# Sliding-window decode attention with a gated feed-forward on one core: TensorE's jumps out, wq in two transfers, four rows of wo moved, a jump announced on VectorE

## The chip, the cores and the metric

The kernel runs on one core of a Trainium2 chip. The metric is the device time of one execution in microseconds (us), lower is better. The profile is of one execution of its own, with its own time.

## The reference

`D` is 448, there are two batch rows (`B`), 16 query heads, 8 key/value heads and a head size of 256. Only the last 2048 rows of the caches are used. Everything in memory is bf16.

```python
def _A_ref(x, k_cache, v_cache, wq, wo):
    ...
    q = (lambda x, *d: x.transpose(*d))((x @ wq).reshape(B, Sq, Hq, Dh), 0, 2, 1, 3)
    k = jnp.repeat(k_cache[:, :, Sk - W:, :], rep, axis=1)
    v = jnp.repeat(v_cache[:, :, Sk - W:, :], rep, axis=1)
    scores = jnp.einsum("bhqd,bhkd->bhqk", q, k) * (Dh ** -0.5)
    p = _softmax(scores, axis=-1)
    o = jnp.einsum("bhqk,bhkd->bhqd", p, v)
    return (lambda x, *d: x.transpose(*d))(o, 0, 2, 1, 3).reshape(B, Sq, Hq * Dh) @ wo
...
xn = _layernorm(x, axis=-1)
s = _A_ref(xn, A_k_cache, A_v_cache, A_wq, A_wo)
g = _silu(_B_ref(xn, B_w1, B_w2))     # relu(xn @ w1) @ w2
return x + s * g
```

## The kernel before, in words

The work is 44.1 MB of reading: wq (3.67 MB), w1 and w2 (1.6 MB each), 16.8 MB of keys, 16.8 MB of values and wo (3.67 MB). A tile is always 128 partitions; the weights lie so that each partition gets one contiguous run of the source (`wq_src`, `w1_src`, `w2_src`, `wo_src`, L234 to L237). wo's partition p holds rows 32p to 32p+31 of the matrix, so a "row j" below means one row of 448 elements (896 bytes) in each of the 128 partitions.

**Order of the work.** A small recorder, `_Prog`, collects operations in five lists, one for each engine, with the operations that each depends on. `run` (L43) writes the lists out and turns dependences into semaphore waits. An engine's order is the order of the calls; nothing else plans it. All operations pass through `op` and `dma`, so the trace gives L39 for transfers and L294 for all matmuls.

**SyncE** issues all large transfers, in this order: wq (L241), w1, w2, the four key blocks of 4.2 MB (`d_k`, L245, `u` = 0 to 3), then the value blocks (`load_v`, L460). A value block goes into the same buffer `kv[u]` as the keys, so it waits for the last score matmul of that block (`last_S[u]`). The fourth one is cut in halves (L481 and L482). Last comes wo in five pieces of 20, 4, 4, 3 and 1 rows (`WO_PARTS`, L147; issued at L500) into `wqo`, the buffer that held wq. **ScalarE's queue** issues the three small loads of x (`x_sb` at L231, `x_c` at L233), before ScalarE's own work.

**Start.** VectorE makes the layernorm from `x_sb` (L254 to L291); TensorE turns it (`mbk`, L297) and VectorE writes `xr` (L300). TensorE multiplies with wq (`qbk`, L305 to L311). VectorE and TensorE bring the queries into `qstat` (L312 to L325). Then `do_H` and `do_F` do the feed-forward, and VectorE keeps `g_sb` (L457).

**Middle.** For each block, `do_turn` transposes the keys on VectorE, `do_S` multiplies, `do_max` and the exponential follow, `do_et` transposes. After `do_spread`, `do_PV(u)` multiplies with the values, `do_out` normalises and `do_turn_out` brings the result into `at2`. `fill` (L385) is TensorE work whose result nobody reads.

**End.** Rows 0 to 23 of wo are multiplied into `wbk` with four rows side by side in the array (L505), and VectorE copies the sum (`wc`, L510). Rows 24 to 31 go as four narrow matmuls each into `fbk` (L513); before row 28 (`WO_FOLD`) the sum `wc` is added in (L514 to L518). VectorE multiplies with `g_sb` (L527), adds x (L529), and two stores go out (L531).

**Jumps.** `emit_pe` (L79) cuts TensorE's list at four marks and puts the parts in bodies. TensorE starts with `eng.br("visit1")`, jumps on to `visit3`, from there back to `part0` at the start of its list, then runs the parts in order with a jump between them. A register that is never set decides every conditional jump the same way. `mark_branch_hint_location` and `branch_hint` put an instruction ahead that tells the sequencer of a later jump.

Of the kernel before, what the change touches and what calls it, by code (L numbers as in the profile page):

```python
# [22 lines left out]
class _Prog:  # L23
# [5 lines left out]

    def mark(self, name, more=0):  # L30
        self.marks[name] = len(self.lists[PE]) + more

# [10 lines left out]
    def run(self):  # L43
# [30 lines left out]

        for eng, e in ((nc.sync, SP), (nc.gpsimd, POOL), (nc.scalar, ACTE), (nc.vector, DVE)):
            emit(eng, self.lists[e])
        self.emit_pe(emit)

    def emit_pe(self, emit):  # L79


        nc, eng, ops, seen = self.nc, self.nc.tensor, self.lists[PE], {}
        a, b, c, d = (self.marks[k] for k in ("block1", "block2", "block3", "late"))

        def body(name):
            return nc.body(name, valid_engines=[eng.engine])

        zero = eng.alloc_register("never_set")
        eng.br("visit1")
        with body("part0"):  # L90
            emit(eng, ops[:a], seen)
            eng.br("part1")
        with body("visit1"):
            eng.reg_mov(zero, 0)
            told_visit = eng.mark_branch_hint_location()
            eng.br("visit3")
        with body("part1"):
            emit(eng, ops[a:b], seen)
            told_late = eng.mark_branch_hint_location()
            emit(eng, ops[b:c], seen)  # L100
            eng.br("part3")
        with body("visit3"):
            eng.br_eq(zero, 0, "part0", "part3").branch_hint(told_visit)
        with body("part3"):
            emit(eng, ops[c:d], seen)
            eng.br_eq(zero, 0, "late", "over").branch_hint(told_late)
        with body("over"):
            eng.br("late")
        with body("late"):
            eng.br_eq(zero, 0, "part4", "past")  # L110
        with body("past"):
            eng.br("part4")
        with body("part4"):
            emit(eng, ops[d:], seen)


def bass_recurrent_scan__sliding_block_cached__dense_activation_relu__decode_kernel(
# [28 lines left out]
    PADW = 5  # L146
    WO_PARTS = [20, 4, 4, 3, 1]  # L147
    WO_TILED = 24
    WO_FOLD = 28

    es = contextlib.ExitStack()
    with es:
        pr = _Prog(nc, es)

        def named(name, shape, dt):
            return es.enter_context(nc.sbuf_tensor(name, shape, dt))
# [56 lines left out]
        o_odd = named("o_odd", [128, DH], F32)  # L213
        at2 = named("at2", [128, 32 * PADW], BF)

        sbk = [psum(f"sbk{i}", [128, 512], F32) for i in range(2)]
# [7 lines left out]
        def half(t, h):  # L224
            return t.rearrange("b s (k h n) -> h (b s k) n", h=2, n=NCOL)[h]
# [4 lines left out]

        d_x = pr.dma(ACTE, x_sb[0:B, :], A_x[:, 0, :])  # L231
        p_xc = pr.op(POOL, lambda e: e.memset(x_c[:, :], 0.0))
        d_xc = [pr.dma(ACTE, x_c[32 * h:32 * h + 4, :], half(A_x, h), [p_xc]) for h in range(2)]  # L233
        wq_src = A_wq.rearrange("r (hf c) -> (r hf) c", hf=2).rearrange("(p s) c -> p (s c)", s=SLOTS)  # L234
# [5 lines left out]
        st = {}  # L240
        d_wq = pr.dma(SP, wqo[:, 0:SLOTS * HC], wq_src)  # L241
        st["w1"] = pr.dma(SP, w1_sb[:, :], w1_src)
        st["w2"] = pr.dma(SP, w2_sb[:, :], w2_src)
        for u in range(NU):
# [6 lines left out]
        p_z = [pr.op(POOL, lambda e, t=t: e.memset(t[:, :], 0.0))  # L251
               for t in (fpad, asel, rm, bt, qstat, at2)][-1]

        v_bn = pr.op(DVE, lambda e: e.bn_stats(st6[0:B, :], x_sb[0:B, :]), [d_x])  # L254
# [8 lines left out]
        def z(t):  # L263
            return a_z[t.name]
# [39 lines left out]

        deps = [d_wq, v_xr, z(qbk)]  # L305
        for s in range(SLOTS):
# [132 lines left out]
        def do_F():  # L439
            deps = [st["w2"], st["h"], z(fbk)]  # L440
            for j in range(14):
                i = j % 4
                o = pr.op(PE, mm(fbk[32 * i:32 * i + B, 0:D], h_sb[:, 32 * j:32 * j + 2], w2_sb[:, j * D:j * D + D],
                                 j < 4, j >= 10, tile_position=(0, 32 * i)), deps)
                deps = []
            v = pr.op(DVE, lambda e: e.tensor_copy(zc[:, :], fbk[:, 0:D]), [o])
            deps = [v, v_fp, st["mbk"]]
# [21 lines left out]
        pr.mark("block1", 16)  # L469
        do_S(1)  # L470
# [17 lines left out]
        for u in range(NU):  # L488
            do_PV(u)
            if u == 0:  # L490
                pr.mark("block2")
# [10 lines left out]
        pr.mark("block3")  # L502
        fill(2)
        deps = [st["at"], z(wbk)]
        for j in range(WO_TILED):  # L505
            i = j % 4
            o = pr.op(PE, mm(wbk[32 * i:32 * i + B, 0:D], view(at2, PADW * j + 1, [[2, B]]), wqo[:, j * D:j * D + D],
                             j < 4, j >= WO_TILED - 4, tile_position=(0, 32 * i)), deps + [landed.get(j)])
            deps = []
        v_wc = pr.op(DVE, lambda e: e.tensor_copy(wc[:, :], wbk[:, 0:D]), [o])  # L510
        pr.mark("late")
        deps = [st["g"]]
        for j in range(WO_TILED, 32):  # L513
            if j == WO_FOLD:  # L514
# [4 lines left out]
            for c in range(4):  # L519
                k, h = divmod(c, 2)  # L520
                lo = j * D + c * NCOL
                m_o = pr.op(PE, mm(fbk[32 * h:32 * h + 4, 0:NCOL], at2[:, PADW * j + 1 - k:PADW * j + 5 - k],
                                   wqo[:, lo:lo + NCOL], j == WO_TILED and k == 0, j == 31,
                                   tile_position=(0, 32 * h)), deps + [landed.get(j)])
                deps = []

        v_t = pr.op(DVE, lambda e: e.tensor_tensor(  # L527
            out=tmp[0:ROWS, :], in0=fbk[0:ROWS, 0:NCOL], in1=g_sb[0:ROWS, :], op=ALU.mult), [m_o, st["g"]])
# [35 lines left out]
```

## Time and profile before

| | us |
|---|---|
| median of 3 runs (109.98 to 110.4) | 110.16 |
| the profiled execution's own time | 110.08 |
| its span, first to last instruction of the program | 108.8 |
| matmuls, busy | 59.0 |
| VectorE, busy | 61.5 |
| ScalarE, busy | 9.0 |
| mean rate read from HBM over the span | 406 GB/s |

Times are counted from the start of the span. Busy shares are averages over stages with different limits: what counts is which wait ends last in a stage. Besides instructions the trace keeps DMA packets (start, duration, size, queue), and for each transfer the moments at which its semaphore rises, one for each of the DMA engines that carry it; a transfer over 128 partitions has sixteen. Packets on queues named "instruction" bring program code to an engine's sequencer: they are not issued by any line of the kernel.

### The profile page before, as it was taken

How to read it: one execution, taken by the hardware profiler on the slowest of the kernel's cores; microseconds unless marked ns; L12 is line 12 of the kernel's file. 1: busy time of each engine (PE TensorE's matmuls, PEld its weight loads, DVE VectorE, ACT ScalarE, POOL GpSimd, SP SyncE). 2: the span in 40 equal slices, each digit the busy share in tenths (PEclk: the TensorE clock that was granted, in tenths of full speed). 3: DMA queues.
4: the chain of work that ended last, by engine and by line, in shares of the span. 5: the costliest groups of instructions: out<-in, count | busy, mean ns of one | idle time of the engine just before them, and what ended most of it. 6: DMA issues, size and time to landing. Idle time of an engine off the chain costs nothing.

```text
span 108.8 us, 1114 instructions
## 1 busy us (share of the span) xinstructions
PE 59.0 (54%) x469; PEld 15.1 (14%) x469; DVE 61.5 (57%) x84; ACT 9.0 (8%) x18; POOL 2.1 (2%) x13
## 2 busy tenths in 40 slices
PE   0001295650000069919961996299538967779672
PEld 0000023120000011001100120012023222313131
DVE  2920007634099979999999999940449332304021
ACT  2970000000000000002000200020020000000000
POOL 7000000000000000000000000000000000000000
PEclk9999999995555558995998599669955699999999
DMA  6899999989998999899999999999999899999960
GB/s 165 337 428 411 409 434 507 407 386 494 458 398 386 494 446 410 386 494 446 410 389 482 446 410 398 470 458 410 398 458 470 362 428 434 434 422 422 397 254 1
DMA packets 2488, 44.17 MB, mean 406 GB/s; under 512 B 306, under 2 KB 436, under 8 KB 820
## 3 DMA queue, kind: packets, MB, share of 16 engines
q1 hardware_dynamic: 2456, 44.11, 95.2%
q8 instruction: 3, 0.05, 0.2%
q10 hardware_dynamic: 28, 0.00, 0.0%
q14 instruction: 1, 0.01, 0.0%
HBM read 44.11 MB, written 0.00 MB: 406 GB/s over the span
## 4 chain that ended last, share of the span: by engine, by line
DMA 56%; DVE 28%; PE 8%; SPq 5%; issue 1%
DMA kv<-in_A_k_cache_dram 32%; DVE kv L329 24%; DMA wqo<-in_A_wo_dram 23%; PE sbk L294 7%; SPq L39 5%; PE fbk L294 1%; DVE q_x L358 1%; DVE rm L346 1%; DVE rm_t L348 0%; DVE bias L352 0%; DVE bt L349 0%; DVE tmp L527 0%; DVE out_sb L529 0%
## 5 line engine op out<-in xcount | busy, mean ns | idle before, releaser
L294 PE MATMUL sbk<-kv,qstat 128*8 128x512 bf16 x128 | 30.2, 1092 | 22.9 <-DVE kv L329 22.9
L329 DVE STREAM_TRANSPOSE kv<-kv 128x2048 f32<-128x2048 f32 x16 | 35.6, 2276 | 4.6 <-DMA kv<-in_A_k_cache_dram 4.6
L294 PEld LDWEIGHTS sbk<-kv,qstat 128*8 128x8 bf16 x128 | 4.5, 107 | 46.9 <-DVE kv L329 28.9
L294 PE MATMUL obk<-kv,pt 128*16 128x512 bf16 x128 | 9.5, 442 | 2.5 <-DVE xg L410 1.2
L407 DVE TENSOR_SCALAR o_odd<-obk,rs 128x256 f32<-128x256 f32 x4 | 1.9, 484 | 11.0 <-PE obk L294 11.0
L353 ACT ACTIVATE e_sb<-sbk,bias 128x512 bf16<-128x512 f32 x4 | 2.8, 688 | 51.9 <-DVE bias L352 51.9
L294 PE MATMUL sbk<-kv,f 128*8 128x512 f32 x14 | 6.9, 612 | 0.0
L294 PE MATMUL qbk<-wqo,xr 128*4 128x512 bf16 x28 | 3.2, 625 | 4.2 <-DMA wqo<-in_A_wq_dram 4.2
L346 DVE TENSOR_REDUCE rm<-sbk 128x1 f32<-128x512 f32 x4 | 2.7, 663 | 4.8 <-PE sbk L294 4.8
L294 PE MATMUL mbk<-ident,xg 2*128 2x2 bf16 x7 | 0.3, 160 | 8.5 <-issue 8.5
L312 DVE TENSOR_SCALAR q_x<-qbk 128x512 bf16<-128x512 f32 x1 | 0.7, 691 | 7.1 <-PE qbk L294 7.1
L294 PEld LDWEIGHTS obk<-kv,pt 128*16 128x16 bf16 x128 | 3.2, 97 | 8.5 <-issue 5.0
L358 DVE STREAM_TRANSPOSE q_x<-e_sb 128x512 bf16<-128x512 bf16 x4 | 2.8, 692 | 1.7 <-ACT e_sb L353 1.7
L375 DVE TENSOR_TENSOR pt<-spk,pmask 128x512 bf16<-128x512 f32 x4 | 2.6, 684 | 0.8 <-PE spk L294 0.8
L510 DVE COPY wc<-wbk 128x448 f32<-128x448 f32 x1 | 0.6, 625 | 3.8 <-PE wbk L294 3.8
L294 PE MATMUL qbk<-w_sb,xr 128*2 128x448 bf16 x28 | 2.8, 572 | 0.0
L294 PE MATMUL spk<-q_x,perm 128*32 128x128 bf16 x16 | 0.7, 298 | 3.1 <-DVE q_x L358 3.1
L323 DVE CAST qstat<-mbk 32x256 bf16<-32x256 f32 x4 | 1.7, 420 | 0.7 <-PE mbk L294 0.7
L410 DVE SCALAR_TENSOR_TENSOR xg<-obk,rs,o_odd 128x256 bf16<-128x256 f32 x4 | 1.9, 484 | 0.1
L294 PE MATMUL wbk<-wqo,at 128*2 128x448 bf16 x24 | 1.4, 351 | 1.0 <-DMA wqo<-in_A_wo_dram 1.0
L254 DVE BATCH_NORM_STATS2 st<-x_sb 2x6 f32<-2x448 bf16 x1 | 0.6, 615 | 2.1 <-DMA x_sb<-in_A_x_dram 2.1
L294 PE MATMUL fbk<-w_sb,h_sb 128*2 128x448 bf16 x14 | 0.9, 351 | 1.5 <-issue 1.5
(72 smaller groups left out, 33.4 us busy)
## 6 DMA issues: line engine op xcount, KB each, us to landing
kv<-in_A_k_cache_dram SPq DMA_DIRECT2D x4, 4096.0 KB, 39.7
kv<-in_A_v_cache_dram SPq DMA_DIRECT2D x3, 4096.0 KB, 22.2
kv<-in_A_v_cache_dram SPq DMA_DIRECT2D x2, 2048.0 KB, 17.5
wqo<-in_A_wq_dram SPq DMA_DIRECT2D x1, 3584.0 KB, 12.2
w_sb<-in_B_w_dram SPq DMA_DIRECT2D x2, 1568.0 KB, 17.0
wqo<-in_A_wo_dram SPq DMA_DIRECT2D x1, 2240.0 KB, 24.3
wqo<-in_A_wo_dram SPq DMA_DIRECT2D x2, 448.0 KB, 25.1
wqo<-in_A_wo_dram SPq DMA_DIRECT2D x1, 336.0 KB, 25.8
```

Source lines behind the costliest of these rows:

```text
L39: o = _Op(eng, lambda e: e.dma_start(dst, src), [d for d in deps if d is not None], True)
L254: v_bn = pr.op(DVE, lambda e: e.bn_stats(st6[0:B, :], x_sb[0:B, :]), [d_x])
L294: return lambda e: e.matmul(out_ap, lhsT=lhsT, rhs=rhs, start=start, stop=stop, skip_group_check=True, **kw)
L312: v_q = pr.op(DVE, lambda e: e.tensor_scalar(out=view(q_x, 0, [[256, 8], [128, 2], [1, 32]]), in0=view(qbk, 0, [[64, 8], [1, 2], [2, 32]]) ...
L323: st["q"] = st["mbk"] = pr.op(DVE, lambda e, Q=Q: e.tensor_copy(qstat[32 * Q:32 * Q + 32, 256 * Q:256 * Q + 256], mbk[32 * Q:32 * Q + 32, ...
L329: st["turn", u] = pr.op(DVE, lambda e, n=n: e.transpose(kf[:, 2048 * n:2048 * n + 2048], kf[:, 2048 * n:2048 * n + 2048]), [d_k[u]])
L346: v = pr.op(DVE, lambda e: e.tensor_reduce(out=rm[:, 0:1], in_=sbk[u % 2][:, :], axis=AX.X, op=ALU.max), [last_S[u], p_z, st.get(("rmt", u ...
L353: st["exp", u] = pr.op(ACTE, lambda e: e.activation(e_sb[:, :], sbk[u % 2][:, :], ACT.Exp, bias=bias[:, 0:1], accum_out=ssum[:, u:u + 1]), ...
L358: st["et", u] = pr.op(DVE, lambda e: e.transpose(q_x[:, 512 * u:512 * u + 512], e_sb[:, :]), [st["exp", u], m_qt])
L375: st["pt", u] = pr.op(DVE, lambda e: e.tensor_tensor(out=view(pt[u], 0, [[8, 64], [2, 4], [1, 2]]), in0=view(spk, 128 * u, [[2, 64], [0, 4 ...
L407: v = pr.op(DVE, lambda e: e.tensor_scalar(out=o_odd[:, :], in0=obk[:, DH:2 * DH], scalar1=rs[:, 2 * u + 1:2 * u + 2], scalar2=None, op0=A ...
L410: st["osb", u] = pr.op(DVE, lambda e: e.scalar_tensor_tensor(out=o_sb[:, lo:lo + DH], in0=obk[:, 0:DH], scalar=rs[:, 2 * u:2 * u + 1], in1 ...
```

## The change

- **TensorE** loses all jumps; its list is written out straight. `emit_pe` is gone.
- **wq** comes by two transfers: slots 0 to 3 from SyncE, slots 4 to 6 from ScalarE's queue. The second is now first in ScalarE's queue, and the loads of x come behind it.
- **wo**: of the 32 rows of each partition the first 28 stay in `wqo`, in pieces of 18, 4, 3, 2 and 1. The last four go into partitions 32 to 79 of three places: those of source partitions 0 to 47 to a free part of `wqo`, 48 to 95 to `w1_sb`, 96 to 127 to `w2_sb` (48, 48 and 32 partitions of 3584 bytes). These three transfers are issued ahead of the rest of wo. Their other operand, `atx`, is made from `at2` by three matmuls with 0/1 matrices (`move`) and a copy. The matmuls with them (12, three for each four rows) come first in `wbk`. Rows 0 to 21 follow there; rows 22 to 27 go the narrow way, with the fold before row 25.
- **VectorE** makes `move` with three copies after `do_F`, announces a jump right behind them, before the first `do_turn`, and jumps between its last `wc` copy and its last two operations. GpSimd clears `move`.

```diff
-    def mark(self, name, more=0):
-        self.marks[name] = len(self.lists[PE]) + more
+    def mark(self, name):
+        self.marks[name] = len(self.lists[DVE])
...
-        for eng, e in ((nc.sync, SP), (nc.gpsimd, POOL), (nc.scalar, ACTE), (nc.vector, DVE)):
+        for eng, e in ((nc.sync, SP), (nc.gpsimd, POOL), (nc.scalar, ACTE), (nc.tensor, PE)):
             emit(eng, self.lists[e])
-        self.emit_pe(emit)
+        self.emit_dve(emit)
+    def emit_dve(self, emit):
+        nc, eng, ops, seen = self.nc, self.nc.vector, self.lists[DVE], {}
+        a, b = self.marks["tell"], self.marks["jump"]
+        emit(eng, ops[:a], seen)
+        zero = eng.alloc_register("never_set")
+        eng.reg_mov(zero, 0)
+        told = eng.mark_branch_hint_location()
+        emit(eng, ops[a:b], seen)
+        eng.br_eq(zero, 0, "last", "past").branch_hint(told)
+        with nc.body("past", valid_engines=[eng.engine]):
+            eng.br("last")
+        with nc.body("last", valid_engines=[eng.engine]):
+            emit(eng, ops[b:], seen)
...
-    WO_PARTS = [20, 4, 4, 3, 1]
-    WO_TILED = 24
-    WO_FOLD = 28
+    WO_PARTS = [18, 4, 3, 2, 1]
+    WO_ALL = sum(WO_PARTS)
+    WO_EXTRA = 32 - WO_ALL
+    WO_MOVED = ((0, 12), (48, 12), (96, 8))
+    WO_TILED = 22
+    WO_FOLD = 25
...
-        d_wq = pr.dma(SP, wqo[:, 0:SLOTS * HC], wq_src)
+        d_wq = [pr.dma(eng, wqo[:, lo * HC:hi * HC], wq_src[:, lo * HC:hi * HC])
+                for eng, lo, hi in ((SP, 0, 4), (ACTE, 4, SLOTS))]
+        d_x = pr.dma(ACTE, x_sb[0:B, :], A_x[:, 0, :])
+        d_xc = [pr.dma(ACTE, x_c[32 * h:32 * h + 4, :], half(A_x, h), [p_xc]) for h in range(2)]
...
+            if hg == 0:
+                return
+            deps = [st["at"], v_mv]
+            for x in range(len(WO_MOVED)):
+                at_x = 352 + x * WO_EXTRA * B
+                o = pr.op(PE, mm(mbk[:, at_x:at_x + WO_EXTRA * B], move[:, 128 * x:128 * x + 128],
+                                 view(at2, PADW * WO_ALL + 1, [[PADW, WO_EXTRA], [2, B]]), True, True), deps)
+                deps = []
+            st["atx"] = st["mbk"] = pr.op(DVE, lambda e: e.tensor_copy(
+                atx[:, :], mbk[:, 352:352 + len(WO_MOVED) * WO_EXTRA * B]), [o])
...
+        for x, (q, nq) in enumerate(WO_MOVED):
+            v_mv = pr.op(DVE, lambda e, x=x, q=q, nq=nq: e.tensor_copy(
+                view(move, 128 * x + 32, [[4, nq], [1, 4]]), view(ident, q, [[1, nq], [nq, 4]])), [p_id, p_mv])
+        pr.mark("tell")
...
+        moved = [t[:, lo:lo + WO_EXTRA * D] for t, lo in ((wqo, WO_ALL * D), (w1_sb, 0), (w2_sb, 0))]
         landed, j0 = {}, 0
         for n in WO_PARTS:
+            if j0 == 0:
+                for x, (q, nq) in enumerate(WO_MOVED):
+                    src = wo_src[q:q + 4 * nq, WO_ALL * D:].rearrange("(r q) c -> q r c", r=4)
+                    landed["x", x] = pr.dma(SP, moved[x][32:32 + 4 * nq, :], src, [m_q, st["h"], st["f"]])
             landed[j0] = pr.dma(SP, wqo[:, j0 * D:(j0 + n) * D], wo_src[:, j0 * D:(j0 + n) * D], [m_q])
```

More of the change, by code (lines that the diff above doesn't have):

```diff
@@ L73, in emit @@
                     made.then_inc(o.sem, 16 if o.dma else 1)
-        for eng, e in ((nc.sync, SP), (nc.gpsimd, POOL), (nc.scalar, ACTE), (nc.vector, DVE)):
+        for eng, e in ((nc.sync, SP), (nc.gpsimd, POOL), (nc.scalar, ACTE), (nc.tensor, PE)):
             emit(eng, self.lists[e])
-        self.emit_pe(emit)
[L79 to L86, printed above, removed]
-        zero = eng.alloc_register("never_set")
[L89 to L114, printed above, removed]
+        self.emit_dve(emit)
[3 more added lines that the diff above has]
+        emit(eng, ops[:a], seen)
+        zero = eng.alloc_register("never_set")
+        eng.reg_mov(zero, 0)
[6 more added lines that the diff above has]
+            emit(eng, ops[b:], seen)
 def bass_recurrent_scan__sliding_block_cached__dense_activation_relu__decode_kernel(
@@ L214, in bass_recurrent_scan__sliding_block_cached__dense_activation_relu__decode_kernel @@
         at2 = named("at2", [128, 32 * PADW], BF)
+        atx = named("atx", [128, len(WO_MOVED) * WO_EXTRA * 2], BF)
+        move = named("move", [128, len(WO_MOVED) * 128], BF)
         sbk = [psum(f"sbk{i}", [128, 512], F32) for i in range(2)]
@@ L229, in kv_src @@
             return cache[b, 4 * hg:4 * hg + 4, SK - W:SK, :].rearrange("g (p t) d -> p g (t d)", t=NT)
-        d_x = pr.dma(ACTE, x_sb[0:B, :], A_x[:, 0, :])
         p_xc = pr.op(POOL, lambda e: e.memset(x_c[:, :], 0.0))
-        d_xc = [pr.dma(ACTE, x_c[32 * h:32 * h + 4, :], half(A_x, h), [p_xc]) for h in range(2)]
         wq_src = A_wq.rearrange("r (hf c) -> (r hf) c", hf=2).rearrange("(p s) c -> p (s c)", s=SLOTS)
@@ L252, in bass_recurrent_scan__sliding_block_cached__dense_activation_relu__decode_kernel @@
                for t in (fpad, asel, rm, bt, qstat, at2)][-1]
+        p_mv = pr.op(POOL, lambda e: e.memset(move[:, :], 0.0))
         v_bn = pr.op(DVE, lambda e: e.bn_stats(st6[0:B, :], x_sb[0:B, :]), [d_x])
@@ L302, in bass_recurrent_scan__sliding_block_cached__dense_activation_relu__decode_kernel @@
             in1=view(par8, 0, [[1, SLOTS], [1, 2], [0, 2]]), op=ALU.mult), [m_xr, v_par8])
-        deps = [d_wq, v_xr, z(qbk)]
+        deps = d_wq + [v_xr, z(qbk)]
         for s in range(SLOTS):
@@ L445, in do_F @@
                 deps = []
+            st["f"] = o
             v = pr.op(DVE, lambda e: e.tensor_copy(zc[:, :], fbk[:, 0:D]), [o])
@@ L468, in bass_recurrent_scan__sliding_block_cached__dense_activation_relu__decode_kernel @@
         do_turn(1, 0, 4)
-        pr.mark("block1", 16)
         do_S(1)
@@ L489, in bass_recurrent_scan__sliding_block_cached__dense_activation_relu__decode_kernel @@
             do_PV(u)
-            if u == 0:
-                pr.mark("block2")
             if u in (0, NU - 1):
@@ L496, in bass_recurrent_scan__sliding_block_cached__dense_activation_relu__decode_kernel @@
                 do_turn_out(u - 2)
+        moved = [t[:, lo:lo + WO_EXTRA * D] for t, lo in ((wqo, WO_ALL * D), (w1_sb, 0), (w2_sb, 0))]
         landed, j0 = {}, 0
         for n in WO_PARTS:
+            if j0 == 0:
+                for x, (q, nq) in enumerate(WO_MOVED):
+                    src = wo_src[q:q + 4 * nq, WO_ALL * D:].rearrange("(r q) c -> q r c", r=4)
+                    landed["x", x] = pr.dma(SP, moved[x][32:32 + 4 * nq, :], src, [m_q, st["h"], st["f"]])
             landed[j0] = pr.dma(SP, wqo[:, j0 * D:(j0 + n) * D], wo_src[:, j0 * D:(j0 + n) * D], [m_q])
             j0 += n
-        pr.mark("block3")
         fill(2)
-        deps = [st["at"], z(wbk)]
-        for j in range(WO_TILED):
-            i = j % 4
-            o = pr.op(PE, mm(wbk[32 * i:32 * i + B, 0:D], view(at2, PADW * j + 1, [[2, B]]), wqo[:, j * D:j * D + D],
-                             j < 4, j >= WO_TILED - 4, tile_position=(0, 32 * i)), deps + [landed.get(j)])
+        rows = []
+        for x in range(len(WO_MOVED)):
+            for j in range(WO_EXTRA):
+                k = B * len(rows)
+                rows.append((atx[:, k:k + B], moved[x][:, j * D:j * D + D], landed["x", x]))
+        for j in range(WO_TILED):
+            rows.append((view(at2, PADW * j + 1, [[2, B]]), wqo[:, j * D:j * D + D], landed.get(j)))
+        deps = [st["at"], st["atx"], z(wbk)]
+        for k, (lhsT, rhs, d) in enumerate(rows):
+            i = k % 4
+            o = pr.op(PE, mm(wbk[32 * i:32 * i + B, 0:D], lhsT, rhs, k < 4, k >= len(rows) - 4,
+                             tile_position=(0, 32 * i)), deps + [d])
             deps = []
         v_wc = pr.op(DVE, lambda e: e.tensor_copy(wc[:, :], wbk[:, 0:D]), [o])
-        pr.mark("late")
         deps = [st["g"]]
-        for j in range(WO_TILED, 32):
+        for j in range(WO_TILED, WO_ALL):
             if j == WO_FOLD:
@@ L522, in bass_recurrent_scan__sliding_block_cached__dense_activation_relu__decode_kernel @@
                 m_o = pr.op(PE, mm(fbk[32 * h:32 * h + 4, 0:NCOL], at2[:, PADW * j + 1 - k:PADW * j + 5 - k],
-                                   wqo[:, lo:lo + NCOL], j == WO_TILED and k == 0, j == 31,
+                                   wqo[:, lo:lo + NCOL], j == WO_TILED and k == 0, j == WO_ALL - 1,
                                    tile_position=(0, 32 * h)), deps + [landed.get(j)])
                 deps = []
+        pr.mark("jump")
         v_t = pr.op(DVE, lambda e: e.tensor_tensor(
```

## The prediction

> **What bounds the kernel now.** I read the page first: the slices, the DMA queues, the chain.
>
> ```profile
> span 108.8 us, 1114 instructions
> ...
> DMA  6899999989998999899999999999999899999960
> ...
> q1 hardware_dynamic: 2456, 44.11, 95.2%
> q8 instruction: 3, 0.05, 0.2%
> ...
> q14 instruction: 1, 0.01, 0.0%
> ```
>
> The DMA digits are 8 or 9 from the second slice to the 38th: SyncE's queue (q1) keeps its sixteen engines busy for 95.2% of the span, and TensorE and VectorE only have to keep up. They do: each value block is issued (46.48, 56.17, 66.93, 77.57) some 10 us before the queue has worked off what is ahead of it. Packet by packet the trace shows the same: a 32768-byte packet takes 1.213 us with no gap behind it on every engine. So the end is set by bytes per DMA engine, and by the last engine, not the mean one.
>
> Then the start and the end of the timeline (start, duration, engine):
>
> ```profile
> 2.08 0.61 DVE L254 BATCH_NORM_STATS2 st<-x_sb 2x6 f32<-2x448 bf16 x1 [2.08 <-DMA x_sb<-in_A_x_dram]
> ...
> 8.84 0.19 DVE L300 TENSOR_TENSOR xr<-mbk,par 128x28 bf16<-128x28 f32 x1 [2.67 <-PE mbk L294]
> ...
> 12.96 3.16 PE L294 MATMUL qbk<-wqo,xr 128*4 128x512 bf16 x28 [4.16 <-DMA wqo<-in_A_wq_dram]
> ```
>
> ```profile
> 104.62 0.62 DVE L510 COPY wc<-wbk 128x448 f32<-128x448 f32 x1 [3.82 <-PE wbk L294]
> ...
> 105.34 0.56 PE L294 MATMUL fbk<-wqo,at 128*4 128x112 bf16 x16 [0.78 <-DMA wqo<-in_A_wo_dram]
> ...
> 105.73 0.55 PE L294 MATMUL fbk<-wc,fpad 128*4 128x112 f32 x8
> ...
> 106.19 0.56 PE L294 MATMUL fbk<-wqo,at 128*4 128x112 bf16 x16
> 106.79 0.27 DVE L527 TENSOR_TENSOR tmp<-fbk,g_sb 36x112 f32<-36x112 f32 x1 [1.54 <-PE fbk L294]
> ```
>
> At the start, x is there at 2 and wq at 12.9. At the end TensorE waits for pieces of wo, and all that follows is a tail of 2.4 us.
>
> The semaphore of the last piece of wo rises sixteen times: thirteen engines between 104.94 and 105.52, then 105.79, 106.22 and 106.39. Three are late because they also carried program code. Two carried TensorE's (16384 bytes at 1.93 in 1.48 us, at 5.79 in 0.96); the packet behind each took 1.53 instead of 1.06. On wq these two were 0.8 and 1.0 late already, and kept that. The third carried 8192 bytes at 54.79 (0.31 us, next packet 1.74 instead of 1.21: 0.84 lost). A last 16384 bytes came at 105.62, when they no longer hurt. Laid end to end the packets tell something of the engines: the two small loads of x_c, four partitions each, ran on the same four engines. The one late from 54.79 is one of those four; the two of TensorE's code are not.
>
> **Part by part**, against the profiled execution's 110.08 (0.08 below the median of 110.16).
>
> *TensorE's jumps out.* Seven jumps (318, 6607, 256, 178, 190, 218 and 349 ns), one move and two hints go. Gain: 0. The 6.6 us jump hides under the wait for wq at 12.96, the last two under waits for wo. What moves is the code: TensorE gets it where it reaches it. The second body began at 48.7; its end, and with it the next block, was due at about 85, the last at 100. From jump to going on took 6.6 us under a full queue, and there are 36 and 15 us of cover: 0, and at most 6.6 without it. The engines pay as before: 0.96 plus 0.47 for each block. If the one of 105.62 is asked for at 100, one more engine pays 1.4.
>
> *wq in two.* The bytes are the same. SyncE's first issue took 0.41 us and its first packets began at 1.76, 1.0 after it; ScalarE's queue began at 1.66, so both start together. The first packets took 1.70 to 2.32 instead of 1.07: two queues could hide up to 0.65 of that; or, if a change of queue costs what it cost behind the code blocks, lose 0.5. The row nearest is x_c, which alternated with wq at no cost (next packet 1.08): 0, with both ends kept. That the first packets are 16384 bytes instead of 28672 narrows their spread: engines ended the first packet between 3.53 and 4.10, that 0.58 stayed to the end (104.94 to 105.52), and 0.57 of it is 0.33.
>
> *x behind wq.* x_sb now waits in ScalarE's queue behind eight packets of 12288 bytes an engine (0.46 each), which alternate with eight of 16384 (0.61): 1.77 + 0.65 + 8 × 1.07 = 11.0, then two packets of w1 at 0.47 and 0.3 for the semaphore: 12.2 instead of 2.06. From x to `xr` there are 3.4 us of instructions without their waits (0.61, 0.17, 0.14, 0.20, 0.14, 1.26, the matmuls, 0.19, gaps): 15.6. The wq matmuls start at 15.7 instead of 12.96, 2.7 late; `g_sb` ends at 28.9 instead of 26.2. The three copies for `move` (0.26 each, the row of `perm`) end at 29.7. The first `do_turn` began at 30.02, when the last, late engine had landed the keys; the others landed by 29.07. So it begins about 29.8: 0. Without this cover, VectorE's chain still has the 10 us ahead of the value loads. GpSimd's clearing (0.36 by the row of `qstat`) meets nothing.
>
> *Moved rows.* Loads of two, four and 128 partitions ran on two, four and sixteen engines. Sources of 12, 12 and 8 outer steps should then run on 12, 12 and 8, that is four packets of 3584 bytes for each engine and transfer. Until now each engine had eight of them for these rows, at 0.136 us. So eight engines get four more (+0.55), four keep theirs, and four lose all eight (-1.09). The Trainium skill, "DMA: Bandwidth & Descriptors", section "Why a DMA increments its semaphore by 16 and not by 1", gives the rule: the largest count up to 16 that divides the slowest dimension of both sides, and the lowest-numbered engines; the two loads of x agree with it (two and four engines), and no run yet shows a twelve. If all sixteen shared instead, the end would stay where it is.
> The sum: unloaded engines that carried code end at 106.39 - 1.09 = 105.30. Loaded ones end at 104.94 plus their own offset (0 to 0.33, 0.2 taken) plus 0.55 plus 0.03 for three more completions: 105.72. The last landing goes from 106.39 to 105.72, a gain of 0.67. This takes the two TensorE engines to be among the relieved four; of twelve engines that they can be, these are the only ones where the edit pays.
>
> *The moved rows on the engines.* Behind the last `at2` copy (ends 100.8) stand three matmuls (0.2); the fills, four matmuls at 0.43, wait for them and end at 102.7 instead of 102.1; the copy `atx` (0.33) is done by 101.4. Twelve rows take three rounds of four at 0.19, to 103.3. The first big piece has landed by then (twelve rows behind it took 3.31, ten take 2.76: 105.72 - 2.76 = 103.0); its 18 rows and the next four, landed at 104.05, take 5.5 rounds, and the last matmul 0.35: 104.7. `wc` ends at 105.3. Rows 22 to 24 have gone through by then; the fold takes 0.46, the last three rows 0.29, the last matmul 0.21: 106.25. Before, the last matmul ended 0.36 after the last landing, now 0.5: the tail gives back 0.1. If `wc` comes 0.3 later, so does the end: this is now the nearest thing behind the landing.
>
> *VectorE's jump.* The 8 KB at 54.79 would sit on an engine that now also carries 0.55 more: 105.79 + 0.58 = 106.37, no gain at all. TensorE's second hint (82.55) was followed by no code packet until its jumps at 104.21 and 104.5, so I take an announced jump to keep the next block away till then. The jump itself took 0.18 to 0.35 in the rows above; VectorE idles 1.54 before L527, so 0. In the Trainium skill, "Runtime: NRT & Kernel Launch", section "Instruction fetch mechanics", a taken branch out of the resident window waits for a fetch, and straight code does not. The 6.6 us jump shows such a wait here; by the rule VectorE would pay at its last jump, a rival below.
>
> Sum: -0.67 + 0.1 = -0.57: 110.08 to **109.5**.
>
> **The rivals.**
> - *Both queues start faster*: another 0.3 to 0.65 off, 109.0. For it: the slow first packets. Against: the engine with two kinds of packets at 1.93 was slower at both.
> - *The code comes to VectorE anyway, or sixteen engines share the moved rows*: the last landing stays at 106.37, 110.1.
> - *The relief falls on the wrong engines* (slower): TensorE's code on an engine with +0.55: 106.39 + 0.58 = 106.97, so 110.7. The same if the third block is fetched at 100 on a loaded engine. It decides as soon as one of the code engines lies among the eight. For: nothing in the trace names the two, only that they are not of the first four.
> - *VectorE's last jump waits for code* (slower): asked at about 105.4, 1.1 until the packet (104.5 to 105.62 on TensorE), 0.31, and 1.25 from packet to going on (6.75 to 8.0): 108.1 instead of 106.4, so 111.2. It decides once the wait exceeds 1.0. For: the 6.6 us jump. Against: six other jumps at 0.18 to 0.35.
> - *Each change of queue in wq costs 0.47* (slower): eight times, 3.8, so 113.3. Against: x_c.
>
> **How the numbers follow.** Forecast 0.50, with its own range of 109.2 to 109.8; 0.35 of it lies below 109.5, roughly 0.5% under the time before (0.5% is about what a measurement of this kernel can tell from no change), 0.15 above. Faster start 0.15. No change 0.08. Wrong engines 0.10, VectorE's jump 0.12, queues 0.05. Faster 0.50, within 0.5% 0.23, slower 0.27. The range goes from 108.9 to 111.2: it leaves out the queues, half of the jump's case, and a little below.
>
> **What the profile would show.** The last piece of wo should rise with no engine more than 0.6 behind the middle one, and last at about 105.7. No 8 KB packet near 54; TensorE's code at about 50 and 85, with no wait of TensorE behind it. wq matmuls at about 15.7, first transpose before 30.1. L527 within 0.5 of the last landing. Wrong: a code packet on an engine that ends last; a first packet rate unlike before; VectorE's last branch over 0.4; the transposes starting after 31.

## The result, and the profile after

The changed kernel takes **110.71 us** (median of 17 executions) beside 110.24 of the kernel before (17 executions): a ratio of 1.0031, 95% interval 1.0017 to 1.0046. The forecast was 109.5, half a per cent faster; measured is 0.3% slower, within what was called no change, and inside the range. One of the seventeen executions took 111.90, more than 1.5% above the fastest, and is left out of the ratio, which is therefore smaller than that of the two medians. The profiled execution takes 110.79, 0.71 more than that of before.

From the page of the changed kernel:

```profile
span 109.5 us, 1127 instructions
...
DMA  4999999899989998999899899989998999999940
...
q1 hardware_dynamic: 2616, 42.53, 90.7%
q10 hardware_dynamic: 172, 1.58, 4.0%
q8 instruction: 3, 0.05, 0.2%
```

The DMA engines are as full as before. q10 is ScalarE's half of wq. The line of q14, VectorE's 8192 bytes, is gone: its announced jump did keep that block away. q8 still carries three blocks for TensorE, at other times (packets, trace): 30.88, 74.22 and **94.23**, before 1.93, 5.79 and 105.62.

The start, from the timeline (start, duration, engine, line):

```profile
12.00 0.62 DVE L240 BATCH_NORM_STATS2 st<-x_sb 2x6 f32<-2x448 bf16 x1 [12.00 <-DMA x_sb<-in_A_x_dram]
...
16.53 0.19 DVE L286 TENSOR_TENSOR xr<-mbk,par 128x28 bf16<-128x28 f32 x1 [0.44 <-PE mbk L280]
...
16.97 3.16 PE L280 MATMUL qbk<-wqo,xr 128*4 128x512 bf16 x28 [0.48 <-DVE xr L286]
```

x is 10 us later, as worked out. The matmuls with wq come 4.0 later (2.7 had been worked out), and no longer wait for wq but for `xr`.

The end:

```profile
104.43 1.44 PE L280 MATMUL wbk<-wqo,at 128*2 128x448 bf16 x22 [0.77 <-DMA wqo<-in_A_wo_dram]
...
105.93 0.62 DVE L519 COPY wc<-wbk 128x448 f32<-128x448 f32 x1 [4.42 <-PE wbk L280]
...
106.31 0.46 PE L280 MATMUL fbk<-wqo,at 128*4 128x112 bf16 x12 [0.44 <-DMA wqo<-in_A_wo_dram]
...
106.61 0.55 PE L280 MATMUL fbk<-wc,fpad 128*4 128x112 f32 x8
...
106.99 0.47 PE L280 MATMUL fbk<-wqo,at 128*4 128x112 bf16 x12
107.49 0.27 DVE L536 TENSOR_TENSOR tmp<-fbk,g_sb 36x112 f32<-36x112 f32 x1 [0.94 <-PE fbk L280]
```

The first tiled rows of the main piece wait until 104.43 for one engine. The last step but one of VectorE (L536, formerly L527) starts at 107.49 instead of 106.79, 0.70 later: that is the whole loss. The semaphore of the last piece of wo shows where it comes from:

| last piece of wo | before | forecast | after |
|---|---|---|---|
| fifteen engines by | 106.22 | | 105.94 |
| the last engine | 106.39 | 105.72 | 107.12 |
| from there to L527 / L536 | 0.40 | 0.5 | 0.37 |

Fifteen engines are nearly where they were meant to be; one lands 1.2 behind them. The transfers of the moved rows name it. Their semaphores rise twelve, twelve and eight times as data lands, and in each exactly one engine is 1.2 to 1.3 behind the next (98.51, 99.04, 99.58). Since it takes part in all three, it is one of the eight that carry more than before, called loaded below. Its packets join without a gap: code at 94.23 (0.88), the next 16384 bytes in 1.16, the next in 0.61, then the moved rows. In the last half block of values, just ahead of them, three engines are late (97.87 to 97.98, the middle one 96.46). The two of the blocks at 30.88 and 74.22 are not late in any moved row: they are among the four that carry none of them, called relieved below.

### The profile page after: what moved, and what is told of

It reads as the page before. It is cut to its first block, busy times and chain, and to the rows that moved or that the text cites. A ratio compares the mean times of both kernels' runs of the same rounds, so it can differ in the third digit from the quotient of the medians.

```text
span 109.5 us, 1127 instructions
## 1 busy us (share of the span) xinstructions
PE 60.5 (55%) x474; PEld 16.5 (15%) x474; DVE 61.8 (56%) x88; ACT 9.0 (8%) x18; POOL 2.5 (2%) x14
## 4 chain that ended last, share of the span: by engine, by line
DVE 44%; DMA 31%; PE 17%; SPq 3%; issue 3%; ACTq 0%; ACT 0%; DVEq 0%
DVE kv L315 32%; DMA wqo<-in_A_wo_dram 21%; DMA x_sb<-in_A_x_dram 10%; PE sbk L280 7%; PE qbk L280 5%; SPq L39 3%; PE fbk L280 3%; PE mbk L280 2%; DVE rm L332 2%; DVE xg L273 1%; DVE q_x L344 1%; DVE tmp L453 1%; DVE q_x L298 1%; DVE rm_t L334 1%; DVE bias L338 1%
## 5 line engine op out<-in xcount | busy, mean ns | idle before, releaser
L280 PE MATMUL sbk<-kv,qstat 128*8 128x512 bf16 x128 | 29.8, 1078 | 18.6 <-DVE kv L315 18.6
L280 PEld LDWEIGHTS sbk<-kv,qstat 128*8 128x8 bf16 x128 | 5.1, 107 | 42.0 <-DVE kv L315 24.8
L280 PEld LDWEIGHTS obk<-kv,pt 128*16 128x16 bf16 x128 | 3.7, 97 | 7.8 <-issue 5.0
L280 PE MATMUL fbk<-w_sb,h_sb 128*2 128x448 bf16 x14 | 1.7, 566 | 1.5 <-issue 1.5
```

Source lines behind the costliest of these rows:

```text
L280: return lambda e: e.matmul(out_ap, lhsT=lhsT, rhs=rhs, start=start, stop=stop, skip_group_check=True, **kw)
```

## The experiments

**Theory A**: taking out TensorE's jumps let the third code block come at 94 instead of 105.6; it fell on one of the eight loaded engines, and that engine sets the end. Rivals: the end is late for another part of the change (wq, VectorE's jump, the moved rows themselves), or for a longer tail. "Last landing" is the last rise of the semaphore of wo's last piece, and "V" the start of VectorE's last step but one, both in the profiled execution. Each ratio is to the kernel before on the same chip; the row "before" has the median of the first comparison.

| kernel | median | ratio (95%) | TensorE's code blocks | last landing | V |
|---|---|---|---|---|---|
| before | 110.24 | | 1.93, 5.79, 105.62 | 106.39 | 106.79 |
| changed | 110.71 | 1.0031 (1.0017 to 1.0046) | 30.88, 74.22, 94.23 | 107.12 | 107.49 |
| e1, jumps back | 112.10 | 1.0183 (1.0150 to 1.0216) | 1.93, 6.10, 105.52 | 105.76 | 108.52 |
| e2, before, jumps out | 110.45 | 1.0017 (1.0003 to 1.0032) | 25.86, 74.26, 93.69 | 106.53 | 106.89 |
| e3, before, rows moved | 112.68 | 1.0216 (1.0192 to 1.0240) | 1.93, 5.70, 106.20 | 106.44 | 109.06 |
| e4, before, wq in two | 110.20 | 1.0003 (0.9989 to 1.0016) | 1.92, 5.92, 105.81 | 106.55 | 106.90 |
| e5, no VectorE jump | 110.95 | 1.0053 (1.0024 to 1.0081) | 31.01, 74.24, 93.58 | 107.08 | 107.46 |
| e7, jumps back, fewer fillers | 111.58 | 1.0142 (1.0106 to 1.0178) | 1.90, 6.12, 106.07 | 105.83 | 107.93 |
| e9, one jump, fewer fillers | 112.41 | 1.0179 (1.0145 to 1.0212) | 29.55, 74.80, 107.33 | 105.94 | 109.19 |
| e10, jumps back, 24 rows tiled | 110.02 | 0.9991 (0.9977 to 1.0004) | 1.96, 6.04, 106.56 | 105.78 | 106.71 |
| e11, jumps back, two rows moved | 110.93 | 1.0068 (1.0053 to 1.0082) | 1.94, 6.39, 107.13 | 106.50 | 107.50 |
| e12, one jump, 24 rows tiled | 110.27 | 1.0013 (1.0000 to 1.0026) | 29.58, 74.50, 106.33 | 105.78 | 106.73 |
| e13, two rows moved | 110.58 | 1.0045 (1.0020 to 1.0070) | 29.81, 74.37, 94.08 | 107.30 | 107.69 |
| e14, e10, other pieces | 110.95 | 1.0043 (1.0020 to 1.0066) | 2.40, 6.37, 106.29 | 106.01 | 106.72 |
| e15, e12, other pieces | 110.85 | 1.0053 (1.0027 to 1.0079) | 30.75, 74.77, 106.59 | 106.35 | 107.00 |

**One part at a time.** e4, the kernel before with wq split:

```diff
-        d_wq = pr.dma(SP, wqo[:, 0:SLOTS * HC], wq_src)
+        d_wq = [pr.dma(eng, wqo[:, lo * HC:hi * HC], wq_src[:, lo * HC:hi * HC])
+                for eng, lo, hi in ((SP, 0, 4), (ACTE, 4, SLOTS))]
```

> The kernel before with wq in two transfers alone, the second one first in ScalarE's queue and x behind it. Theory A: the bytes per engine are the same, the engines with TensorE's code stay last: 110.0 to 110.3; first transpose at about 31.5, without effect on the end. Rival B (the late start costs at the end): 110.5 to 110.8.

Neutral: neither a faster start nor a price for the change of queue. e2, the kernel before without TensorE's jumps:

```diff
-        self.emit_pe(emit)
+        emit(nc.tensor, self.lists[PE])
```

> The kernel before, with nothing changed but that TensorE's jumps are out. Theory A: three code blocks inside the span at about 30 to 95 instead of two at the start, three engines 1.3 to 1.6 behind on wo plus the one of VectorE's code, last landing 106.4 to 106.8, time 110.2 to 110.7. Rival B: 110.2, no difference.

The third block comes at 93.69 here too, but no engine carries more of wo than another, so three are late together (106.44, 106.45, 106.53) and the time hardly moves: 1.0017. Alone, taking the jumps out costs about 0.2%.

e5, the changed kernel without VectorE's jump:

```diff
-        self.emit_dve(emit)
+        emit(nc.vector, self.lists[DVE])
```

> The changed kernel without VectorE's jump and its announcement. Theory A (an announced jump keeps the next code block away): a packet of 8192 bytes comes again at about 55, on an engine with four more packets, 0.85 behind and 0.55 loaded: it ends at about 106.4 and stays behind the engine of TensorE's third block (107.1), so the time is that of the changed kernel, 110.5 to 110.8. Rival B (the announcement itself changes nothing about the code): no 8192-byte packet, 110.5 to 110.8 as well; the packet tells the two apart, not the time.

From its queues:

```profile
q8 instruction: 4, 0.07, 0.2%
q14 instruction: 1, 0.01, 0.0%
```

VectorE's block is back at 54.82 and its engine lands at 106.44 (106.37 had been worked out for that). The last engine is still the one of the block at 93.58, at 107.08. So VectorE's jump does its part, under a later engine. (The median, 110.95, lies a little above the range; V is that of the changed kernel.)

**The jumps back.** e1, the changed kernel with TensorE's jumps of before:

```diff
-        emit(nc.tensor, self.lists[PE])
+        self.emit_pe(emit)
```

> The changed kernel with TensorE's jumps of before put back; wq in two, moved rows and VectorE's jump stay. Theory A (TensorE's last code block, which comes at 94.2 in the changed kernel and came at 105.6 before, loads an engine that also carries four more packets): the last block comes after 104 again, no engine is 1.2 us behind the others on the last piece of wo, the last landing is at 105.8 to 106.2, and the time 109.6 to 109.9. Rival B (the jumps do not matter, the moved rows or the late start cost the time): 110.5 to 110.8, as the changed kernel. Rival A2 (it is the block at 30.9 that sits on a loaded engine): one engine stays 1.2 behind, 110.6.

The landing is what theory A says, 105.76, and no loaded engine is late. But the end went up, which neither expected:

```profile
106.11 0.36 PE L318 MATMUL fbk<-wqo,at 128*4 128x112 bf16 x7
108.17 0.31 PE L318 MATMUL fbk<-wqo,at 128*4 128x112 bf16 x5 [1.70 <-issue]
```

The last five matmuls wait 1.70 us for no data and no semaphore. The code packet of 105.52 ended at 106.7, within that gap: TensorE's list is longer than before, and its last instructions have slid into the next block. (That is a reading of the trace here; e10 below tests it.) e3, the kernel before with nothing but the moved rows, shows the same:

```diff
-    WO_PARTS = [20, 4, 4, 3, 1]
+    WO_PARTS = [18, 4, 3, 2, 1]
+    WO_MOVED = ((0, 12), (48, 12), (96, 8))
```

> The kernel before with the moved rows alone (TensorE's jumps, wq in one and no jump on VectorE). Theory A: the engine of VectorE's 8 KB of code (0.85 behind) is one of those with four more packets, ends at about 106.3, and nothing is gained or lost: 109.9 to 110.3. Rival B (moving the rows costs by itself): 110.5 to 110.8.

```profile
106.29 0.36 PE L300 MATMUL fbk<-wqo,at 128*4 128x112 bf16 x8
...
108.67 0.35 PE L300 MATMUL fbk<-wqo,at 128*4 128x112 bf16 x4 [2.02 <-issue]
```

Its last landing (106.44, the engine with VectorE's block) is as expected and its time is not. So with TensorE's jumps the moved rows alone cost 2%; in the changed kernel, without the jumps, this wait is absent. e7 and e9 make the list shorter by leaving out 4 of the 7 fillers (16 instructions); e9 keeps a single announced jump.

```diff
-            if u in (0, NU - 1):
-                fill(1)
...
-                    fill(3)
+                    fill(1)
```

> The changed kernel with TensorE's jumps of before put back (as in e1_jumps_back) and four of the seven filler products taken out (their result is read by nobody): TensorE's program is 16 instructions shorter. Theory A (in e1_jumps_back the last twelve instructions fell into a code block that came only at 105.5 to 106.7): no wait before the last matmuls, last landing 105.7 to 105.9, last matmul 106.2 to 106.4, time 109.4 to 109.8. Rival C (the wait comes from the jump, not from the place of the block): TensorE waits 1.7 to 2.0 again, 111.9 to 112.3. Rival D (the fillers kept TensorE's clock up): granted clock under 1.0 after 98 and 0.3 to 0.6 more in the tail, 109.8 to 110.4.

> As e7_jumps_shorter, but TensorE has one announced jump alone, as VectorE has: announced behind the first block of values, taken behind the wc copy; no visits at the start. Theory A (the announcement is what keeps the third block away): code at about 31 and 74, the third after 104, last landing 105.7 to 106.0, time 109.4 to 109.8. Rival F (the visits at the start are needed): the third block at about 94 as in the changed kernel, last landing about 107.1, 110.4 to 110.8, or a wait of 6 for a block.

No wait for code is left, and the landings are right (105.83, 105.94), but `wc` starts at 106.36 and 107.62 (105.05 in e1), and neither time lies in a range that was given. The busy times by stretch (length; PE, PEld, DVE, ACT, POOL; then TensorE's clock, DMA share, GB/s) of e7:

```profile
101.00:104.00 3.00, 2.79 (x16) 0.56 (x17) 0.32 (x2) 0.00 (x0) 0.00 (x0) 0.50 0.93 383
```

and of e10, with all fillers:

```profile
101.00:104.00 3.00, 2.85 (x34) 0.94 (x35) 0.26 (x2) 0.00 (x0) 0.00 (x0) 1.00 0.95 387
```

The fillers keep TensorE's granted clock at 1.00 instead of 0.50 in the stretch that counts: e1, which differs from e7 by the fillers alone, has 1.00 there too. That is rival D of e7, at more than twice its price. So e10 keeps them and saves 12 instructions by multiplying rows 22 and 23 in the tiled way, and e12 is the same with one announced jump (`emit_pe` cut down to a hint after the first `do_PV` and a jump at `wc`):

```diff
-    WO_TILED = 22
-    WO_FOLD = 25
+    WO_TILED = 24
+    WO_FOLD = 27
```

> The changed kernel with TensorE's jumps of before, all fillers kept, and TensorE's program made 12 instructions shorter in another way: rows 22 and 23 of wo as two tiled rows (2 instructions each) instead of narrow ones (8 each), the fold ahead of row 27. Theory A (TensorE's third code block, let in at 94 by taking the jumps out, holds the last engine; with the jumps back the last landing is 105.7 to 105.9, and the 2 us wait of the jumps-back run came only from instructions that slid into the next block, 9 or 10 of them): no wait ahead of the last matmuls, TensorE's fills at 0.59 and not 1.06, the last VectorE step but one starting at 106.5 to 106.8 (106.79 before), so 109.8 to 110.1 in all. Rival B (the jumps themselves, or the longer list of rows, cost the tail 2 us wherever the program ends): 111.5 to 112.2 with a wait of TensorE behind issue.

> The changed kernel with one announced jump on TensorE (hint behind the first unit's PV, jump behind wbk's last matmul), all fillers kept, rows 22 and 23 tiled, fold ahead of row 27. Theory A: the announced jump alone keeps the third code block away from 94, so the last landing is 105.75 to 106.0 instead of 107.12; with the fillers TensorE keeps its clock (fills 0.59, rows 0.19 apart), so the end is 109.8 to 110.2 instead of the 112.4 of the one-jump run with fewer fillers. Rival D (the 112.4 came from the jump and not from the missing fillers): 112 or more again, rows of wo slow with all fillers in place.

Landing at 105.78, no wait for code and a clock at 1.00 in both; the times are 110.02, in its range, and 110.27, 0.07 above it. One announced jump is enough to hold the third block off until the jump is taken. Against the changed kernel the last engine is 1.3 earlier, but V only 0.8. The end of e10:

```profile
105.34 0.62 DVE L561 COPY wc<-wbk 128x448 f32<-128x448 f32 x1 [3.75 <-PE wbk L318]
...
106.02 0.55 PE L318 MATMUL fbk<-wc,fpad 128*4 128x112 f32 x8
...
106.41 0.27 PE L318 MATMUL fbk<-wqo,at 128*4 128x112 bf16 x4
106.71 0.27 DVE L579 TENSOR_TENSOR tmp<-fbk,g_sb 36x112 f32<-36x112 f32 x1 [0.75 <-PE fbk L318]
```

The fold comes at 106.02 because `wc` begins at 105.34. The end now waits for `wc`, not for the landing.

**Two rows moved instead of four** (loaded engines +0.27 instead of +0.55), with TensorE's jumps in e11 and without them in e13:

```diff
-    WO_PARTS = [18, 4, 3, 2, 1]
+    WO_PARTS = [20, 4, 3, 2, 1]
...
```

The rows that are multiplied in the tiled way grow with it: 25 in e11 (fold before row 29), 24 in e13 (before row 27).

> The same with two rows of each partition moved instead of four (wo in pieces of 20, 4, 3, 2 and 1 rows, 25 of them tiled, fold ahead of row 29), TensorE's program 14 instructions shorter than in the jumps-back run, all fillers kept. Theory A: loaded engines carry 0.27 more instead of 0.55 and land at 105.4 to 105.5; the two engines of TensorE's first code blocks lose 0.55 instead of 1.09 and land last, at 105.8 to 105.9; no wait behind issue, last VectorE step but one at 106.3 to 106.6, in all 109.6 to 109.9. Rival B (jumps or list of rows cost the tail 2 us): 111.5 to 112. If the fills run at 1.06 instead of 0.59, the price of a slow TensorE clock comes on top (about 1).

> The changed kernel as it is, without TensorE's jumps, but two rows of each partition moved instead of four (pieces of 20, 4, 3, 2 and 1 rows, 24 tiled, fold ahead of row 27). Theory A (the last engine carries the third code block and the added rows, so its lateness is the sum of both): last landing 107.12 - 0.27 = 106.85, the block at 93 to 95, last VectorE step but one about 107.2, in all 110.4 to 110.6. Rival B (lateness of that engine comes from the code block alone and not from the added rows): 107.1 and 110.7 as with four rows. If the program's layout puts the third block after 98 or on another engine, the last landing is 106.0 to 106.6.

e11 missed: one engine lands at 106.50, 0.6 later than worked out, and the time, 110.93, is 1.0 above its range. The engine is a relieved one with a first code block, 2.0 behind the middle before wo (98.39) where 1.6 had been assumed, and two rows relieve it by only 0.55. e13's landing (107.30) missed as well (its time, 110.58, did not); that execution was 0.3 late on all engines at 86 already, so it can't tell A from B. An earlier run, e8, had two rows moved, the jumps and 8 instructions of filler fewer:

> As e7_jumps_shorter, but two rows of wo moved instead of four (30 in wqo, in pieces of 20, 4, 3, 2 and 1), and two fillers out instead of four. Theory A: eight engines get two more packets (0.27), the engines with code lose four (0.55); these end at about 105.3 to 105.5, the loaded ones at about 105.5, last landing 105.4 to 105.6, time 109.1 to 109.6, 0.1 to 0.3 under e7. Rival E (what counts is the mean over the engines, not the last one): 110.0 to 110.3 as before.

It gave 111.00 (ratio 1.0049, 1.0019 to 1.0078), in executions from 109.86 to 113.17. The profiled one is the longest of them; its last landing is 106.53, a miss of the same size as e11's. It settles nothing more.

**The tail through `wc`.** e14 (from e10) and e15 (from e12) move only the borders of the pieces, so that the tiled rows land with a piece of their own:

```diff
-    WO_PARTS = [18, 4, 3, 2, 1]
+    WO_PARTS = [20, 4, 2, 1, 1]
```

> The run with TensorE's jumps back and 24 tiled rows, with one more edit: wo's big loads in pieces of 20, 4, 2, 1 and 1 rows instead of 18, 4, 3, 2 and 1, so that the last tiled rows (22 and 23) are the end of a piece that lands at about 104.65 and not in the middle of one that lands at 104.9. Theory A (the tail goes through wc: the last tiled rows, their 0.4, wc's 0.62, the fold and the last row): wc starts at 105.05 instead of 105.34, the fold at 105.73 instead of 106.02, the last VectorE step but one at 106.4 to 106.5 instead of 106.71, in all 109.75 to 109.9, last landing as before at 105.75 to 105.85. Rival B (what follows the landing sets the end whatever wc does): 106.65 to 106.75 and 110.0 to 110.1. Rival C (smaller last pieces or a first piece that lands later cost as much as they bring): wc at 105.3 or later, 110.0 or more.

> The run with one announced jump on TensorE and 24 tiled rows, with the same pieces of 20, 4, 2, 1 and 1 rows. Theory A: the same 0.25 to 0.3 off the run with one jump (110.27), so 109.95 to 110.05. Rival B: 110.2 to 110.3.

In these profiles the last engines brought the pieces late (106.01, 106.35), `wc` came no earlier than without the edit (105.35, 105.63), and the medians are worse, with executions from 110.01 to 111.38. Both missed theory A; e14 came out as its rival C. A second profile of e14's kernel:

> The run with pieces of 20, 4, 2, 1 and 1 rows once more (110.02 with a last landing at 106.01 in its profiled execution; its other executions reach 111.21). Theory A: in a slower execution one engine lands later by what the time is longer, since a block of code or a slow first packet stayed with it. Rival B: landing near 106.0 and a tail longer by what the time is longer, with TensorE's rows over 0.2 apart.

It took 109.80, with the last engine at 105.85 and the tail that e14's theory A had worked out. As this execution was a short one, it can't tell why others are longer:

```profile
105.13 0.62 DVE L561 COPY wc<-wbk 128x448 f32<-128x448 f32 x1 [3.63 <-PE wbk L318]
...
105.81 0.55 PE L318 MATMUL fbk<-wc,fpad 128*4 128x112 f32 x8
...
106.50 0.27 DVE L579 TENSOR_TENSOR tmp<-fbk,g_sb 36x112 f32<-36x112 f32 x1 [0.75 <-PE fbk L318]
```

V follows `wc` in both profiles of this kernel (1.37 behind). So the gain is there in one execution, and the median doesn't have it. A second profile of e10's kernel:

> The run with TensorE's jumps back and 24 tiled rows once more (110.15 with a last landing at 105.78 in its profiled execution, 109.90 to 110.15 in four). Theory A: 109.9 to 110.4 with the landing at 105.7 to 106.0. Rival B: if it spreads like the others, up to 111, with a tail that is longer.

gave 110.04 with the landing at 105.78, as the first time.

**The changed kernel again, twice.**

> The changed kernel once more, for one profiled execution. Theory A (the third code block comes at 94 in every execution, and its engine sets the end; what spreads is how late that engine is): last landing 106.5 to 107.4, the end 0.3 to 0.5 behind it in every execution, so the time follows the landing one for one (110.79 with 107.12). Rival B (the spread is the tail's: TensorE's clock): landing 107.1 again and the time differs through the tail, fills at over 0.6 or rows over 0.2 apart.

> As the look before it: the changed kernel, one profiled execution more. Theory A: time = 110.79 + (last landing - 107.12), within 0.15. Rival B: landing 107.1, the time differs through the tail.

The first is a copy: block at 94.81, landing 107.09, V 107.47, 110.90. In the second the block came at 93.66, and *no* engine is late in the moved rows (97.17, 97.71, 98.28 at the latest): this time the third engine, too, is one of the four relieved. Theory A, that this block's engine sets the end in every execution, is wrong here. All engines land by 105.86:

```profile
105.08 0.62 DVE L519 COPY wc<-wbk 128x448 f32<-128x448 f32 x1 [3.34 <-PE wbk L280]
...
105.76 0.56 PE L280 MATMUL fbk<-wc,fpad 128*4 128x112 f32 x8 [0.25 <-DVE wc L519]
...
106.14 0.47 PE L280 MATMUL fbk<-wqo,at 128*4 128x112 bf16 x12
106.65 0.27 DVE L536 TENSOR_TENSOR tmp<-fbk,g_sb 36x112 f32<-36x112 f32 x1 [0.94 <-PE fbk L280]
```

The same program, the same block, another engine: 1.23 less at the landing, V 0.82 earlier than in the first of the two and a span of 108.6 instead of 109.4. Theory A's sum would give 109.5 for it; its time was 111.05: 2.45 lie outside the span, where the other two profiles of this kernel have 1.3 and 1.5. A fourth code block of TensorE, at 109.92 for 1.37, comes after the program's last work; e13 has one at 110.02 (0.88) with 1.3 outside the span. What the 2.45 are was not tried.

## Why the prediction was wrong

**The step that failed** is the first one, "TensorE's jumps out. [...] Gain: 0", with "If the one of 105.62 is asked for at 100, one more engine pays 1.4" left out of the sum. TensorE itself did not wait, as worked out, and the price of 1.4 was right; what failed is the term that was put at nothing, the third code block. It came at 94.23, its engine paid 1.4 (0.88 for the block and 0.55 in the next packet), and the engine was a loaded one: 107.12 instead of about 105.7. That is the second half of the rival "the relief falls on the wrong engines", priced at 110.7; measured 110.71, and it had been given 0.10. That the two agree to 0.01 is in part luck, since the executions spread over more than 1 us. Eight of the sixteen engines are loaded, so once the block comes ahead of the end the chance was, as an estimate, nearer to a half. In the five profiles with moved rows and no jumps on TensorE the block fell on a loaded engine four times (changed kernel twice, e5, e13) and once on a relieved one. The dates were also too late: 85 and 100 were due by the counts, 74 and 94 came.

"Gain: 0" was wrong the other way too. With the moved rows, TensorE's list no longer ends ahead of the block that the jumps hold off: with everything else changed and the jumps kept (e1), the kernel takes 112.10 (ratio 1.0183), 1.4 more than the changed one.

The sum had seen that an announced jump holds a code block off: it used this for VectorE. The same row said what taking away TensorE's announcement would do.

Point by point:

- *Moved rows*: right. 12, 12 and 8 engines; e1 has its last landing at 105.76 for 105.72. The count by the rule in the Trainium skill, "DMA: Bandwidth & Descriptors", section "Why a DMA increments its semaphore by 16 and not by 1", is borne out for twelve as well. The two engines of the first blocks were among the relieved in each profile with moved rows. That both lie there had been taken without a row that shows it; of the twelve possible engines four are relieved, so it came right by luck (about one in eleven, an estimate from these counts).
- *VectorE's jump*: right. No 8 KB packet, the jump took 0.078 and so did not wait for code, and e5 puts the engine without it at 106.44.
- *wq in two*: right that it brings no gain and has no price (e4). The narrower spread is not shown: at the first half of the last value block the engines without code lie within 0.57 of each other in the changed kernel (91.45 to 92.02) and 0.56 before, and in e4, which has this edit alone, within 0.90 (91.47 to 92.37).
- *x behind wq*: landing right (12.0 for 12.2), matmuls 1.3 later than worked out (16.97 for 15.7). VectorE's ten small constants (L255 to L269) ran in the shade of other waits before; now they stand behind the waiting `bn_stats`. The sum from x to `xr` took instructions from one path and forgot those queued on the engine. The first `do_turn` starts at 31.54 instead of 29.8, past the 31 that was named as a sign of being wrong. It costs nothing at the end: e4, whose transposes start at 31.37, takes as long as the kernel before.
- *The tail*: mis-sized, +0.4 instead of +0.1. Where the landing was about as forecast (second of the two profiles above, 105.86) V comes 0.79 behind it, before 0.40. There `wc` starts at 105.08 and not at 104.7, and the fold waits for it, as the working had warned. The lines of that profile show why:

```profile
100.89 0.34 DVE L408 CAST at<-mbk 64x64 bf16<-64x64 f32 x1 [0.54 <-PE mbk L280]
...
102.74 0.59 PE L280 MATMUL sbk<-kv,f 128*8 128x512 f32 x1
...
103.17 0.35 PE L280 MATMUL wbk<-wqo,atx 128*2 128x448 bf16 x1
```

The last `at2` copy ends at 101.23 and not at 100.8, so the last fill starts at 102.74 and the fills are through at 103.17 and not at 102.7. Three of each four tiled rows run beside the fills (from 101.89, 102.32 and 102.75); the fourth, at tile position 0, where the fills write as well, starts only at 103.17. Nine rows stand there, 0.19 apart, and the last takes 0.35: 105.04. The copy is late because of the values, not of wo. In eighteen of the twenty profiles (all but e8 and e9) it ends 3.0 us after the last engine has landed the last half block of values, 97.78 before and 98.22 here, and that engine is late by TensorE's code. The moved rows relieve such an engine only afterwards. With this tail the last step but one starts 106.79 - 106.65 = 0.14 earlier than before, not 0.57; e10, where the third block is held off, agrees with 0.08. No run changed the values' landing alone.

So two things stood between what fifteen engines gained (106.39 to 105.94; 0.6 in e1) and the end: a code block on a loaded engine, which made it a loss, and a tail that had no more than 0.1 to 0.3 to give (0.08 in e10, 0.29 in the second profile of e14's kernel).

**Open.** Executions of the changed kernel lie between 110.09 and 111.35, but for the one of 111.90, those of before between 109.98 and 110.47. That the engine of the third block differs between executions is seen in one of three profiles of this kernel, and would give two values; there are times in between, and spans too (108.6 to 109.8). So the cause is shown for the profiled executions, and for the median as far as they stand for it. e14 and e15 spread as far with the third block held off, and none of their longest executions was profiled. No version was shown to beat the kernel before: e10 is equal to it.

## What to carry to other kernels

When the end is set by the last of sixteen DMA engines, a change that loads some engines more and others less also makes the kernel sensitive to where program code lands; list every block that can come before the end and give each its chance of hitting a loaded engine. Before taking out a jump, look which code block it holds off and when that block will come without it; before adding instructions, look how near the last ones are to the next block. And of a gain at the landing, count only what the chain behind it can follow.

## What the runs showed of the hardware

- An announced jump holds the next code block off until it is taken. TensorE's third block came at 93.6 to 94.8 in the six profiles without jumps on TensorE, and at 105.5 to 107.3 in the fourteen with an announced one, 1.4 us after that jump (once 1.6). VectorE's 8192 bytes came at 53.6 to 54.8 in the five profiles without its jump and in none of the fifteen with it. No run has the late jump without its announcement, so which of the two holds the block is not shown.
- The price of that: what lies beyond the block is not there yet. The last matmuls of e1 and e3 stood 1.70 and 2.02 us in a straight run of instructions and went on 1.4 to 1.5 us after the end of a code packet; with a list shorter by 12 (e10) the wait is gone. The Trainium skill, "Runtime: NRT & Kernel Launch", section "Instruction fetch mechanics", has straight code streamed ahead, its price mostly hidden, and a stall at a taken branch out of the window. These waits lie in straight code, behind a jump that had held the fetch up: here the measurement decides.
- An engine that carries a block of 16384 bytes falls behind: at the last half block of values by 0.8 to 2.0 us against the middle engine. The block itself takes 0.9 to 1.0 in the middle of the span (1.3 to 2.1 for the one in the first microseconds), the rest goes into the next packets. Which engine it is was not the same in all executions of one program.
- Taking out 16 instructions of filler halved TensorE's granted clock (0.50 for 1.00) in the stretch ahead of the end and made `wc` 1.3 us later (106.36 in e7, 105.05 in e1, which differ by the fillers alone).
